# Attention beside linear attention: a tile transpose moved from TensorE and VectorE to the DMA engines, with another opening, another closing and one more block of exponentials on VectorE

## The chip, the cores and the metric

The kernel runs on one core of a Trainium2 chip. The metric is the device time of one execution in microseconds (us); the time before is the median of three runs. The profile is of one further execution, which has its own time.

## The reference

Two independent layers read a sequence of 2048 rows of width 640, with 32 heads of width 20, in bf16; their outputs are set side by side.

```python
# A: softmax attention, no mask
q, k, v = split(x @ wqkv)                       # 32 heads of 20
p = softmax(q @ k.T * 20 ** -0.5)               # per head 2048 x 2048
a = concat_heads(p @ v) @ wo
# B: linear attention, phi(t) = where(t > 0, t + 1, exp(t)) + 1e-6
kv, z = phi(k).T @ v, phi(k).sum(0)             # per head 20 x 20 and 20
o = (phi(q) @ kv) / (phi(q) @ z + 1e-6)
b = concat_heads(o) @ wo
out = concat([a, b], -1)                        # 2048 x 1280
```

## The kernel before

**A.** The scores are cut into blocks of 128 keys by 512 queries of one head, written key-major into a PSUM bank. Four heads form a head group (8 of them) and four stretches of 512 queries a sequence, so there are 32 chunks, numbered n; a chunk has 16 key tiles kt of four blocks each, and four blocks of one key tile are a quad. The exponential of a block is done in one of two ways. Most go to ScalarE (`emit_exp`, L1266), which takes three and then two blocks from PSUM in one instruction; each such set is a group, numbered j, and `SB` has the two sets of banks, 0 to 2 and 3 to 4, that it alternates between. The others go to VectorE (`d_score`): a scale per block (L1301), then three polynomial steps for each pair of blocks (L1312, L1316, L1320). The table `ND` says for each chunk how many of its 16 quads VectorE takes; it sums to 56 of 512. `LEAD` says how far ahead of its chunk, in chunk lengths, VectorE begins. The product with V adds up in bank `PVB` over the 16 key tiles of a chunk; `norm` then divides by the row sum and puts the result in `OTp`, from where DMAs on the queue of SyncE (SP) carry it to `OTd`, the operand of the output product.

**B** and all projections are background steps (`_Step`): some matmuls into bank 6 or 7 and an evacuation. In the last part of B each tile t of 128 rows goes through `ndstep` (numerator and denominator of both halves of the heads; VectorE divides, L1719 and L1722, and writes the normalised rows to `o`, a part of tile `f_pk`), `trstep` (five TensorE transposes of 128 x 128 into PSUM, L1734, and one VectorE copy to `oT`, another part of `f_pk`, L1744) and `ostep` (the product of `oT` with `woB`, a part of `f_wBkv`, and the store of the rows).

**Order.** The program is straight-line code. A planner (`_Clock`) runs while it is generated: each operation has a modelled cost, and it picks the order in which steps, scores and VectorE operations are emitted for each engine. On the chip each engine runs its list in that order and waits on semaphores; TensorE in particular takes nothing out of turn. Idle stretches of TensorE are padded with products of zeros (`f_g`, `f_z` in the views), and the start with products of a constant (`warm_up`).

**Opening.** `start_loads` brings the first 512 rows of x as they are (tile `f_st`, two DMAs of 256 rows), pieces of the weights `f_wA`, and the other 1536 rows by DMA transposes from DRAM (15 of 512 x 128). `consts` transposes the first 512 rows on TensorE (L1070), copied to `f_xT` by VectorE and ScalarE. Q and K of the first chunk follow, and then the first scores.

**Closing.** After the last V product, the last `norm` gives `OTp`, which meets the weights of the last head group, `wo7`. The last 512 rows are eight half tiles. For those not in `LATE` the product of the other heads was done before and lies in `part`, added by VectorE (L1550); for those in `LATE`, `part1` puts it in a free bank after the last V product, `part2` adds the last group's share, and ScalarE copies the sum (L1546). The stores go out at L1537.

Of the kernel before, what the change touches and what calls it, by code (L numbers as in the profile page):

```python
# [6 lines left out]
BF16 = mybir.dt.bfloat16  # L7
# [8 lines left out]
D_MODEL = 640  # L16
# [711 lines left out]
class _Clock:  # L728
# [5 lines left out]
    def __init__(self):  # L734
        self.t = {"act": 2.0, "dve": 0.0, "pool": 0.0, "sp": 1.0}
        self.issue = 0.0
        self.mode = None
        self.tile = {}
        self.hist = []
# [60 lines left out]
class _Fast:  # L800
# [11 lines left out]
    LEAD = 0.6  # L812
    LATE = ((3, 1), (3, 0), (2, 1))
    ND = (1, 2, 2, 1, 2, 2, 1, 2, 2, 2, 2, 2, 2, 2, 1, 2, 2, 2, 2, 2, 2, 2, 1, 1, 2, 2, 2, 2, 2, 1, 2, 1)
# [208 lines left out]
    def start_loads(self):  # L1023
# [5 lines left out]
        for k in range(2):  # L1029
            sch.dma("sp", lambda e, k=k: e.dma_start(  # L1030
                xn[:, 2 * k:2 * k + 2, :], x2[256 * k:256 * (k + 1), :].rearrange("(t p) d -> p t d", p=128)),
                writes=tuple(("xn", t) for t in (2 * k, 2 * k + 1)), cost=(0.1, 3.5))
# [3 lines left out]
        def load(q, part):  # L1036
            a, b, res = part
            sch.dma(q, lambda e: e.dma_start(self.wA[:, :, a:b], awq[:, :, a:b]), writes=(res,),
                    cost=(0.5, 5.0 if b - a < 200 else 8.0))
# [3 lines left out]
        load("act", parts[0])  # L1043
        load("act", parts[1])
        load("sp", parts[2])
        for tc in range(1, self.NQC):
            for c in range(N_DC):
                sch.dma("sp", lambda e, c=c, tc=tc: e.dma_start_transpose(
                    self.xT[:, c, 512 * tc:512 * (tc + 1)], x2[512 * tc:512 * (tc + 1), 128 * c:128 * (c + 1)]),
                    writes=(("xT", c, tc),), cost=(1.65, 2.0))  # L1050
# [8 lines left out]
    def consts(self):  # L1059
# [6 lines left out]
        for half in range(2):  # L1066
            for c in range(N_DC):
                pb = ps[:, c, :].bitcast(BF16)
                for t in (2 * half, 2 * half + 1):
                    sch.op("pe", lambda e, c=c, t=t, pb=pb: e.transpose(  # L1070
                        pb[:, 128 * t:128 * (t + 1)], self.stage[:, t, 128 * c:128 * (c + 1)], self.ident[:]),
                        reads=(("xn", t), "ident"), writes=(("ps", c),), inc=(t == 3), cost=("f", 0, 128))
            if half == 0:
                self.warm_up(2)
        self.warm_up(2)
# [53 lines left out]
    def step_qk(self, which, g, tc):  # L1129
# [20 lines left out]
        def post(b):  # L1150
# [5 lines left out]
            if g == 0 and tc == 0 and which == "Q":  # L1156
                return sch.op("act", lambda e: e.copy(dst, ps[:, b, :]), reads=(("ps", b),), writes=(res,),
                              cost=0.5).t
            if which == "K" and tc == 0:
                res = (res, ("K0", g % 2))  # L1160
                if g == 0:
                    self.dve(0.29, lambda e: e.tensor_copy(dst[:, 0:128], ps[:, b, 0:128]), reads=(("ps", b),),  # L1162
                             writes=(("K0", 0),))
                    return self.dve(0.56, lambda e: e.tensor_copy(dst[:, 128:512], ps[:, b, 128:512]),  # L1164
                                    reads=(("ps", b),), writes=(("K", 0, 0),)).t
            else:
                res = (res,)
# [68 lines left out]

    def force_qk(self, n, kt):
        g, qc = divmod(n, self.NQC)
        self.force(("Q", g, qc))
        self.force(("K", g, kt // 4))  # L1240
# [10 lines left out]
    def ahead(self, j):  # L1251
        for n, kt, i in self.groups[min(j + 4, len(self.groups) - 1)]:
            self.force_qk(n, kt)
# [251 lines left out]
    def finish_out(self):  # L1505
# [6 lines left out]
        banks = dict(zip(tiles, (6, 7, 3, 4, self.PVB, 0, 1, 2)))  # L1512

        def part1(x):
            for c in range(N_DC):
                self.out_round(banks[x], t0 + x[0], slice(320 * x[1], 320 * x[1] + 320), c, c == 0, False, True)
# [23 lines left out]
        for k in range(len(tiles) - len(late)):  # L1540
            for x in tiles[k:k + 1] + late[k:k + 1]:
# [43 lines left out]
    def b_steps(self):  # L1585
# [113 lines left out]
        def ndstep(t, h):  # L1699
# [15 lines left out]
            def post(b):  # L1715
# [8 lines left out]
                         writes=(("o", k, h),) + tuple(("pk", tl2, h2) for tl2 in range(4) for h2 in range(2)))  # L1724
            needs = tuple(("bq", tc, c) for c in cs) + (("bkv", NQC - 1, 3),)
            return _Step(mms, post, needs=needs, key=("nd", t, h), cols=2352)

        def trstep(t):
            k = t % 2

            def mms(b):
                pb = ps[:, b, :].bitcast(BF16)
                for c in range(N_DC):
                    sch.op("pe", lambda e, c=c: e.transpose(pb[:, 128 * c:128 * (c + 1)],  # L1734
                                                            self.o[:, k, 128 * c:128 * (c + 1)],
                                                            self.ident[:]),
                           reads=(("o", k, 0), ("o", k, 1), "ident"), writes=(("ps", b),), inc=(c == N_DC - 1),
                           cost=("f", 0, 128))
                    yield 128

            def post(b):
                pb = ps[:, b, :].bitcast(BF16)
                dst = self.oT[:, k].rearrange("p c m -> p (c m)")
# [316 lines left out]
```

## Time and profile before

| | |
|---|---|
| three runs | 870.16, 871.74, 871.98 us; median 871.74 |
| profiled execution | 870.36 us, of which the span is 868.5 |
| ScalarE busy | 850.1 us, 98% of the span |
| VectorE busy | 751.0 us, 86% |
| TensorE busy | 767.9 us, 88% (padding included) |
| first and last exponential on ScalarE | 10.57 to 858.12 us |

Times in the rows count from the start of the span. PE is TensorE's matmuls, PEld its weight loads, DVE VectorE, ACT ScalarE, SP SyncE; a name with q (SPq, ACTq) is the engine's sequencer, which issues DMAs. In a row of the timeline the first two numbers are start and length in us, and the bracket says how long the engine stood idle before it and for whom.

### The profile page before, as it was taken

What the parts mean: (1) busy time and instruction counts of PE and PEld (TensorE: products, weight loads), DVE (VectorE), ACT (ScalarE), POOL (GpSimd) and SP (SyncE); (2) the same over time, 40 slices, a digit from 0 to 9 for tenths busy, and PEclk for the clock granted to TensorE, in tenths of its full rate; (3) what the DMA queues carried; (4) which work ended last, traced back from release to release, by engine and by line L of the source; (5) the groups of instructions that cost most, each with busy time, mean ns of one, the idle gap of its engine ahead of it and who ended that gap; (6) DMA issues with size and microseconds to landing.
All of it is one profiled execution on the core that took longest, in us unless ns stands there. A gap on an engine that the chain in (4) does not pass through costs nothing.

```text
span 868.5 us, 25388 instructions
## 1 busy us (share of the span) xinstructions
PE 767.9 (88%) x11524; PEld 278.2 (32%) x11524; DVE 751.0 (86%) x1036; ACT 850.1 (98%) x790; POOL 50.9 (6%) x54
## 2 busy tenths in 40 slices
PE   8989888888888998888898999889988888899996
PEld 3333333322333333333332333223322332233342
DVE  6798899878989988998989999998779989898973
ACT  6999999999999999999999999999999999999995
POOL 4000000000000000000000000000000000000000
PEclk9999999999999999999999999999999999999999
DMA  6910001000020010000040000200010000001011
GB/s 130 248 44 5 5 6 32 5 6 6 18 59 3 5 36 6 6 3 3 6 73 6 5 13 19 43 5 14 28 32 5 5 22 21 3 4 44 21 45 65
DMA packets 45748, 24.01 MB, mean 28 GB/s; under 512 B 33985, under 2 KB 44993, under 8 KB 45633
## 3 DMA queue, kind: packets, MB, share of 16 engines
q1 hardware_dynamic: 44176, 21.92, 10.5%
q8 instruction: 92, 1.51, 0.8%
q10 hardware_dynamic: 1456, 0.40, 0.2%
q14 instruction: 24, 0.19, 0.1%
HBM read 7.31 MB, written 5.24 MB: 14 GB/s over the span
## 4 chain that ended last, share of the span: by engine, by line
ACT 95%; PE 4%; DVE 0%; issue 0%; ACTq 0%
ACT f_PT L1266 93%; PE ps L179 4%; ACT f_ex L1570 2%; ACT f_st L1546 0%; PE ps L1070 0%; DVE f_T L1414 0%; DVE f_OTp L1431 0%; DVE f_KT L1164 0%; DVE f_Tn L1427 0%; DVE f_OTp L1041 0%; ACTq L1537 0%; DVE f_KT L1162 0%; DVE f_R L1421 0%; DVE f_warm L1040 0%; ACTq L104 0%
## 5 line engine op out<-in xcount | busy, mean ns | idle before, releaser
L1266 ACT ACTIVATE f_PT<-ps 128x1536 bf16<-128x1536 f32 x730 | 841.4, 1423 | 3.6 <-PE ps L179 3.6
L179 PE MATMUL ps<-f_Qr,f_KT 20*128 20x512 bf16 x2048 | 302.6, 385 | 91.6 <-ACT f_PT L1266 82.3
L179 PE MATMUL ps<-f_g,f_z 32*128 32x512 bf16 (+3 forms) x1008 | 208.5, 378 | 0.0
L1301 DVE TENSOR_SCALAR f_W<-ps 128x512 f32<-128x512 f32 x224 | 154.0, 688 | 53.3 <-PE ps L179 50.5
L179 PEld LDWEIGHTS ps<-f_Qr,f_KT 20*128 20x128 bf16 x2048 | 75.0, 91 | 333.3 <-ACT f_PT L1266 315.4
L179 PE MATMUL ps<-f_PT,f_V 128*21 128x512 bf16 x1824 | 180.6, 387 | 0.8 <-ACT f_PT L1266 0.6
L1312 DVE SCALAR_TENSOR_TENSOR f_PL<-f_W 128x1024 f32<-128x1024 uint16 x112 | 136.2, 1216 | 1.1
L1316 DVE SCALAR_TENSOR_TENSOR f_PL<-f_W,f_PL 128x1024 f32<-128x1024 uint16 x112 | 136.0, 1214 | 1.1
L1320 DVE SCALAR_TENSOR_TENSOR f_PD<-f_PL,f_W 128x1024 uint16<-128x1024 f32 x112 | 135.6, 1211 | 0.6
L179 PE MATMUL ps<-f_xT,f_wA 128*32 128x512 bf16 x1280 | 88.9, 381 | 0.0
L1424 POOL TENSOR_TENSOR f_Tn<-f_T,f_R 128x320 bf16<-128x320 f32 x31 | 41.3, 1331 | 782.8 <-DVE f_R L1421 782.8
L179 PEld LDWEIGHTS ps<-f_PT,f_V 128*21 128x21 bf16 x1824 | 44.5, 89 | 101.0 <-issue 97.5
L179 PE MATMUL ps<-f_wBkv,f_xB 128*32 128x320 bf16 x1280 | 60.4, 303 | 0.0
L179 PEld LDWEIGHTS ps<-f_g,f_z 128*32 128x32 bf16 (+1 forms) x1008 | 51.4, 93 | 12.5 <-issue 8.8
L179 PEld LDWEIGHTS ps<-f_xT,f_wA 128*32 128x32 bf16 x1280 | 30.2, 95 | 30.8 <-issue 9.8
L1467 DVE CAST f_st<-ps 128x320 bf16<-128x320 f32 x56 | 27.2, 487 | 13.9 <-PE ps L179 12.7
L179 PEld LDWEIGHTS ps<-f_wBkv,f_xB 128*32 128x32 bf16 x1280 | 31.1, 97 | 18.6 <-issue 5.5
L1570 ACT ACTIVATE f_ex<-ps 128x320 f32<-128x320 f32 (+1 forms) x52 | 36.3, 698 | 0.0
L179 PE MATMUL ps<-f_wBkv,f_pk 128*32 128x320 bf16 x640 | 30.7, 300 | 0.0
L179 PE MATMUL ps<-f_wA,f_OTd 128*32 128x320 bf16 (+1 forms) x640 | 30.6, 301 | 0.1
L179 PE MATMUL ps<-f_wA,f_xT 128*32 128x160 bf16 (+1 forms) x640 | 29.6, 301 | 0.4
L179 PE MATMUL ps<-f_kvm,f_cs 128*32 128x336 bf16 x384 | 29.1, 306 | 0.0
(88 smaller groups left out, 508.6 us busy)
## 6 DMA issues: line engine op xcount, KB each, us to landing
out_dram<-f_st SPq DMA_DIRECT2D x31, 160.0 KB
f_OTd<-f_OTp SPq DMA_DIRECT2D x108, 20.0 KB
f_wBkv<-in_B_wqkv_dram SPq DMA_DIRECT2D x1, 1600.0 KB
f_wA<-in_A_wqkv_dram SPq DMA_DIRECT2D x2, 685.0 KB
f_wBq<-in_B_wqkv_dram SPq DMA_DIRECT2D x1, 800.0 KB
f_wA<-in_A_wo_dram SPq DMA_DIRECT2D x1, 800.0 KB
f_wBkv<-in_B_wo_dram SPq DMA_DIRECT2D x1, 800.0 KB
f_st<-in_A_x_dram SPq DMA_DIRECT2D x2, 320.0 KB
```

The costliest lines, as they stand in the source:

```text
L179: lambda e: e.matmul(out, lhsT, rhs, start=start, stop=stop, tile_position=tp, skip_group_check=sgc),
L1266: sch.op("act", lambda e: e.activation(self.PT[:, s0:s0 + n, :], ps[:, b0:b0 + n, :], AF.Exp, bias=(self.OCT + self.EXP_S) * LN2, scale=sc ...
L1301: self.dve(0.69, lambda e: e.tensor_scalar(dst, ps[:, b, :], cs, cb, op0=ALU.mult, op1=ALU.add), reads=(("ps", b),), writes=(("W", x, h),))
L1312: self.dve(1.24, lambda e: e.scalar_tensor_tensor(pl, lo, self.EXP_A, lo, op0=ALU.add, op1=ALU.mult), reads=rw, writes=(("PL", x),), fill= ...
L1316: self.dve(1.24, lambda e: e.scalar_tensor_tensor(pl, lo, self.EXP_B, pl, op0=ALU.add, op1=ALU.mult), reads=rw, writes=(("PL", x),), fill= ...
L1320: self.dve(1.24, lambda e: e.scalar_tensor_tensor(pd, pl, self.EXP_K, w, op0=ALU.mult, op1=ALU.add), reads=rw + (("PL", x),), writes=(("PD ...
L1424: sch.op("pool", lambda e: e.tensor_tensor(n3[:, :, 0:D_HEAD], t3[:, :, 0:D_HEAD], rb, op=ALU.mult), reads=("T1", ("R", n % 2)), writes=(" ...
L1467: self.dve(0.49, lambda e: e.tensor_copy(dst, src), reads=reads, writes=writes)
L1570: sch.op("act", lambda e: e.activation(ex, src, AF.Exp, bias=-1.0), reads=(("ps", b),), writes=(("ex", k),), cost=0.05 + 0.00084 * n)
```

## The change

Six edits:

1. `trstep` is gone. When VectorE has written the second half of `o` for a tile, five DMA transposes of 128 x 128 are issued on SP's queue, from `o` to `oT`, both in on-chip memory. `ostep` waits for each fifth by itself. The planner reckons 0.4 us of SP's queue for each and 2.5 us until it has landed.
2. `ND` sums to 57: one more quad goes to VectorE, 4 blocks fewer to ScalarE. Chunk 0 has none now, and chunk 4 has three. `LEAD` is 0.75.
3. The loads at the start are spread: the second half of the first x rows on ScalarE's queue, the piece of K's weights on SP's, the piece of V's weights behind two of the transposes.
4. The four `warm_up` products between and behind the first transposes are gone, and these run by column block.
5. A function `opening` writes the first projections out: all of Q, then the first 128 keys of K, part of the other keys, the scores of group 0, then the rest.
6. `LATE` has four half tiles. All four `part1` come ahead of the `part2`, and the last copies and stores alternate between VectorE and ScalarE.

```diff
-    LATE = ((3, 1), (3, 0), (2, 1))
-    ND = (1, 2, 2, 1, 2, 2, 1, 2, ...
+    LATE = ((3, 1), (3, 0), (2, 1), (2, 0))
+    ND = (0, 2, 2, 1, 3, 2, 0, 2, ...
...
-        for k in range(2):
-            sch.dma("sp", lambda e, k=k: e.dma_start(
+        for k, q in enumerate(("sp", "act")):
+            sch.dma(q, lambda e, k=k: e.dma_start(
...
-        load("act", parts[0])
-        load("act", parts[1])
-        load("sp", parts[2])
+        load("act", parts[0], 2.5)
+        load("sp", parts[1], 3.6)
...
+    def opening(self):
+        rounds("wq", "Q", 6, 0, 512, range(N_DC))
+        self.done[("Q", 0, 0)] = sch.op("act", lambda e: e.copy(self.Qr[:, 0, :], ps[:, 6, :]), ...
+        rounds("wk", "K", 7, 0, 128, range(N_DC))
+        kt = self.KT[:, 0, 0:512]
+        self.dve(0.29, lambda e: e.tensor_copy(kt[:, 0:128], ps[:, 7, 0:128]), ...
+        rounds("wk", "K", 5, 128, 512, range(2))
+        self.emit_scores(0)
+        rounds("wk", "K", 5, 128, 512, range(2, N_DC))
+        self.done[("K", 0, 0)] = self.dve(0.56, lambda e: e.tensor_copy(kt[:, 128:512], ps[:, 5, 128:512]), ...
...
-        for x in late[:2]:
-            part1(x)
-        for x in tiles[:len(tiles) - len(late)]:
-            part2(x)
-        for x in late[:2]:
-            part2(x)
-        for x in late[2:]:
-            part1(x)
-            part2(x)
+        for x in late:
+            for c in range(N_DC):
+                self.out_round(banks[x], t0 + x[0], ...
+        for x, y in zip(tiles, late):
+            part2(x)
+            part2(y)
...
-        def trstep(t):
...
+        def transpose(t):
             k = t % 2
+            for c in range(N_DC):
+                sch.dma("sp", lambda e, c=c: e.dma_start_transpose(
+                    self.oT[:, k, c, :], self.o[:, k, 128 * c:128 * (c + 1)]),
+                    reads=(("o", k, 0), ("o", k, 1)), writes=(("oT", k, c),), cost=(0.4, 2.5))
+            self.done[("tr", t)] = self.ck.t["sp"] + 2.5
...
-            order = [("n", 0), ("n", 1), ("t", 0), ("n", 2), ("o", 0), ("t", 1), ("n", 3), ("o", 1),
-                     ("t", 2), ("o", 2), ("t", 3), ("o", 3)]
+            order = [("n", 0), ("n", 1), ("o", 0), ("n", 2), ("o", 1), ("n", 3), ("o", 2), ("o", 3)]
```

Three places in the order of TensorE's instructions. In them `f_xT,f_wA` is a projection of Q or K, `f_Qr,f_KT` a score block, `f_PT,f_V` and `f_PD,f_V` the product with V of blocks from ScalarE and from VectorE. The first place is the start of the program, before:

```order
L179 MATMUL ps<-f_OTp 128x512 x8
L1070 MATMUL ps<-f_id,f_st 128x128 x10
L179 MATMUL ps<-f_OTp 128x512 x2
L1070 MATMUL ps<-f_id,f_st 128x128 x10
L179 MATMUL ps<-f_OTp 128x512 x2
L179 MATMUL ps<-f_xT,f_wA 32x512 x40
L179 MATMUL ps<-f_Qr,f_KT 128x512 x5
```

The same place with the change:

```order
L179 MATMUL ps<-f_OTp 128x512 x8
L1069 MATMUL ps<-f_id,f_st 128x128 x20
L179 MATMUL ps<-f_xT,f_wA 32x512 x20
L179 MATMUL ps<-f_xT,f_wA 32x128 x20
L179 MATMUL ps<-f_xT,f_wA 32x384 x8
L179 MATMUL ps<-f_Qr,f_KT 128x512 x3
L179 MATMUL ps<-f_xT,f_wA 32x384 x12
L179 MATMUL ps<-f_Qr,f_KT 128x512 x2
```

The scores of the first group (x3) now stand behind 20 + 20 + 8 projections, of which 28 are short, and no longer behind 40 long ones. The second place is in B's last part with the change, around the first matmul of `ostep` for tile t = 3 (`f_wBkv,f_pk` is the output product, its first x8 row that of tile 2, its x16 row that of tile 3):

```order
L179 MATMUL ps<-f_wBkv,f_pk 32x320 x20
L179 MATMUL ps<-f_Qr,f_KT 128x512
L179 MATMUL ps<-f_g,f_z 128x512
L179 MATMUL ps<-f_Qr,f_KT 128x512 x2
L179 MATMUL ps<-f_wBkv,f_pk 32x320 x8
L179 MATMUL ps<-f_Qr,f_KT 128x512
L179 MATMUL ps<-f_g,f_z 128x512
L179 MATMUL ps<-f_Qr,f_KT 128x512
L179 MATMUL ps<-f_PT,f_V 21x512 x4
L179 MATMUL ps<-f_wBkv,f_pk 32x320 x16
```

No transpose stands on TensorE any more; the x16 row waits for DMAs, and scores for ScalarE stand right behind it. Counted over the whole list, the score blocks between the last `ndstep` matmul of a tile and its first `ostep` matmul are, for t = 0 to 15: 19, 34, 50, 16, 22, 49, 33, 28, 19, 34, 46, 17, 28, 36, 102 and 113 (of 2048 in the program). The third place is the closing, before:

```order
L179 MATMUL ps<-f_PT,f_V 21x512 x8
L179 MATMUL ps<-f_wA,f_OTd 32x320 x40
L179 MATMUL ps<-f_wo,f_OTp 32x320 x28
L179 MATMUL ps<-f_wA,f_OTd 32x320 x20
L179 MATMUL ps<-f_wo,f_OTp 32x320 x4
```

The same place with the change:

```order
L179 MATMUL ps<-f_wA,f_OTd 32x320 x20
L179 MATMUL ps<-f_PT,f_V 21x512 x8
L179 MATMUL ps<-f_wA,f_OTd 32x320 x80
L179 MATMUL ps<-f_wo,f_OTp 32x320 x32
```

Between the last V product and the first use of `OTp` stand 80 matmuls now, not 40.

More of the change, by code (lines that the diff above doesn't have):

```diff
@@ L1511, in finish_out @@
         tiles = [x for x in tiles if x not in late] + late
[L1512 to L1516, printed above, removed]
+        last = (len(self.groups) - 1) % 2
+        lb = tuple(self.SB[1 - last]) + tuple(self.SB[last])
+        banks = dict(zip(tiles, (6, 7, self.PVB, lb[4]) + lb[:4]))
         def part2(x):
```

95 lines of the change are left out of this document (41 added, 54 removed).

## The prediction

> **What bounds the kernel now.** The page comes first: the busy times, the chain that ended last, and the costliest group.
>
> ```profile
> PE 767.9 (88%) x11524; PEld 278.2 (32%) x11524; DVE 751.0 (86%) x1036; ACT 850.1 (98%) x790; POOL 50.9 (6%) x54
> ACT 95%; PE 4%; DVE 0%; issue 0%; ACTq 0%
> L1266 ACT ACTIVATE f_PT<-ps 128x1536 bf16<-128x1536 f32 x730 | 841.4, 1423 | 3.6 <-PE ps L179 3.6
> ```
>
> ScalarE works for 98% of the span and is 95% of the chain, nearly all of it in the 730 exponentials. Before them it was idle for only 3.6 us. So three things can move the end: when the first exponential starts, how much ScalarE has to do until the last, and what follows the last. The chain in order of time gives the three stages and the price of a group (the mean of eight, alternating three and two blocks).
>
> ```profile
> 10.57 6.89 ACT f_PT L1266 x6
> 453.44 9.04 ACT f_PT L1266 x8
> 810.88 47.24 ACT f_PT L1266 x42
> 858.12 0.04 issue
> ```
>
> The opening takes 10.57 us, the stream of exponentials 847.5, the closing 868.5 - 858.1 = 10.4. A group costs 9.04 / 8 = 1.13 us for 2.5 blocks, so a block costs 0.452 us. A matmul or a VectorE operation that is removed is worth something only where ScalarE waits for it.
>
> **The opening.** The timeline of its first 11 us:
>
> ```profile
> 0.74 0.97 SPq L1030 DMA_DIRECT2D f_st<-in_A_x_dram  x2
> 1.49 3.40 PE L179 MATMUL ps<-f_OTp 128*128 128x512 bf16 x8 [1.49 <-DVE f_OTp L1041]
> 4.72 0.72 PE L1070 MATMUL ps<-f_id,f_st 128*128 128x128 bf16 x10
> 5.61 0.65 PEld L1070 LDWEIGHTS ps<-f_id,f_st 128*128 128x128 bf16 x10 [0.23 <-DMA f_st<-in_A_x_dram]
> 5.71 0.72 PE L1070 MATMUL ps<-f_id,f_st 128*128 128x128 bf16 x10
> 6.80 2.34 PE L179 MATMUL ps<-f_xT,f_wA 128*32 128x512 bf16 x40
> 8.11 0.59 ACT L1157 CAST f_Qr<-ps 128x512 bf16<-128x512 f32 x1 [0.90 <-PE ps L179]
> 9.52 0.56 DVE L1164 CAST f_KT<-ps 128x384 bf16<-128x384 f32 x1
> 10.13 0.60 PE L179 MATMUL ps<-f_Qr,f_KT 20*128 20x512 bf16 x5 [0.99 <-DVE f_KT L1164]
> 10.57 17.50 ACT L1266 ACTIVATE f_PT<-ps 128x1536 bf16<-128x1536 f32 x15 [1.87 <-PE ps L179]
> ```
>
> The second half of x landed at about 5.6. Its transposes, 40 projections (all of Q and K) and the copy of the remaining 384 keys then follow one another, and TensorE stands idle for 0.99 us until the copy ends at 10.08. With the change the first group needs only the first 128 keys, since chunk 0 gives no block to VectorE. Group 0 so waits for Q's copy and a copy of 128 columns.
>
> When do the x rows land? The stretches by microsecond, whose last number is GB/s:
>
> ```profile
> 2.00:3.00 1.00, 1.00 (x4) 0.33 (x3) 1.00 (x1) 0.23 (x2) 1.00 (x2) 1.00 0.75 186
> 3.00:4.00 1.00, 1.00 (x3) 0.29 (x2) 0.88 (x1) 0.00 (x0) 1.00 (x4) 1.00 1.18 323
> 4.00:5.00 1.00, 1.00 (x8) 0.57 (x7) 0.00 (x0) 0.00 (x0) 1.00 (x6) 1.00 1.09 312
> ```
>
> Both halves are 655 KB. At 186 + 323 KB by 4.0 and 312 KB per us after that they need until about 4.5 us if nothing is ahead of them, which two queues with x first in each come near to (estimate). Where the weights still share the engines it stays at 5.6. From 4.72 on, 20 transposes take (0.72 - 0.22) / 9 = 0.056 us each (0.22 is the pipeline's own length) and end at 6.0; copies overlap them but for the last, so Q starts at 6.2. Half of 2.34 us later, at 7.45, ScalarE copies Q (0.59, to 8.15 with the wake-up). The 128-key projections and their copy end about then too. As before, 0.44 us lie between the score matmuls and the exponential (10.13 to 10.57): 8.2 + 0.44 = 8.6. With x at 5.6 it is 9.6. I take 8.8, nearer to the early end because x is first in both queues: **-1.8 us** (bounds -2.0 and -1.0). Against that, group 1 needs the remaining keys. Their last 12 matmuls run behind the first scores (8.8 + 0.5), then comes the 0.56 us copy and the scores again, some 10.45, while exponential 0 ends at 8.8 + 1.34: **+0.3 us**. The DMA transposes of the other rows come out no later than before, since only short issues are ahead of them.
>
> **The stream.** `ND` 57 for 56 takes four blocks from ScalarE, 4 x 0.452 = **-1.8 us**. What VectorE takes on and gives up:
>
> ```profile
> L1301 DVE TENSOR_SCALAR f_W<-ps 128x512 f32<-128x512 f32 x224 | 154.0, 688 | 53.3 <-PE ps L179 50.5
> L1312 DVE SCALAR_TENSOR_TENSOR f_PL<-f_W 128x1024 f32<-128x1024 uint16 x112 | 136.2, 1216 | 1.1
> L1722 DVE TENSOR_TENSOR f_pk<-ps,f_rd 128x320 bf16<-128x320 f32 x32 | 15.7, 492 | 1.1
> L1719 DVE RECIPROCAL f_rd<-ps 128x16 f32<-128x16 f32 x32 | 8.0, 250 | 2.0 <-PE ps L179 1.7
> L1744 DVE COPY f_pk<-ps 128x640 bf16<-128x640 bf16 x16 | 7.7, 484 | 1.7 <-PE ps L1734 1.7
> L1734 PE MATMUL ps<-f_id,f_pk 128*128 128x128 bf16 x80 | 8.3, 222 | 0.0
> ```
>
> A quad is 4 x 0.688 and three steps for two pairs, 6 x 1.216: 10.0 us. The 16 copies give back 7.7. VectorE gains 2.3 us on 868.5 - 751 = 117 us of idle time, which covers it: 0 in the sum. TensorE loses 80 transposes of its own padded time: 0 as well.
>
> The new wait is that of `ostep` on its DMAs, and TensorE takes nothing out of turn: behind its first matmul stand the scores of the next groups, and ScalarE has one group (1.13 us) at most before it waits too. No row shows a 128 x 128 transpose within the chip. The nearest are the transposes of B's rows from DRAM, the transposes of the opening, and the small on-chip copies of `OTp` (issue times least/median/most, ns; then one burst of five and the stretches in which its transfers end):
>
> ```profile
> L1558 SPq DMA_TRANSPOSE f_xB<-in_B_x_dram x40: 1132/1261/2198, 28.3 to 633.5; - x40
> L1443 SPq DMA_DIRECT2D f_OTd<-f_OTp x140: 554/707/1088, 42.9 to 839.3; - x140
> 2.26 21.19 SPq L1048 DMA_TRANSPOSE f_xT<-in_A_x_dram  x15
> 128.88 6.37 SPq L1558 DMA_TRANSPOSE f_xB<-in_B_x_dram  x5
> 136.00:136.50 0.50, 0.50 (x20) 0.20 (x12) 0.00 (x0) 0.50 (x2) 0.00 (x0) 1.00 0.35 71
> 136.50:137.00 0.50, 0.50 (x13) 0.15 (x12) 0.09 (x1) 0.50 (x2) 0.00 (x0) 1.00 0.00 0
> ```
>
> The burst was issued by 135.25 and moved its last bytes before 136.5, so a transpose lands 1.25 us after its issue. An issue of ours costs between 0.32 (a quarter of 1.26, being a quarter of the rows) and 1.41 (21.19 / 15). I take 0.8, near the on-chip copies, the only rows with that source. All five so land 5 x 0.8 + 1.25 = 5.25 us after `o` is ready, with 2.9 and 8.3 as ends.
>
> How long may they take? A score block stands for 847.5 / 2048 = 0.414 us of the stream. The tightest tile (t = 3) has 16 of them, 6.6 us, of which VectorE needs about 2.1 (one 1.2 us operation ahead, 0.25 + 0.49 for the division, the wake-ups); the fifth chunk of `oT` is read 0.6 later (a product of five chunks takes 0.9, see the closing). That leaves 5.1 us; the others among the five tightest (17, 19, 19, 22 blocks) have 5.5, 6.4, 6.4 and 7.6. At 5.25 the delay of 0.15 lies inside ScalarE's one group; I put **+0.3 us** for all tiles (bounds 0 and the slow rival's price below).
>
> For a 128 x 128 transpose the Trainium skill, "VectorE: DVE Perf Modes", section "The three transpose paths", gives 390 ns on TensorE and 1309 ns on the DMA path, and its rules advise TensorE where the destination may be PSUM. It speaks against this edit. By its price five in a row take 6.5 + 1.25 = 7.8 us, and the edit would cost about 4 us and not 0.3 (estimate from that page). No row of before decides it; the 1.26 us of a transpose four times as long makes me doubt it.
>
> **The closing.** Its rows:
>
> ```profile
> 858.16 0.59 PEld L179 LDWEIGHTS ps<-f_wA,f_OTd 128*32 128x32 bf16 x16
> 859.02 0.64 PEld L179 LDWEIGHTS ps<-f_wA,f_OTd 48*32 48x32 bf16 x20 [0.26 <-issue]
> 860.92 1.13 PE L179 MATMUL ps<-f_wo,f_OTp 128*32 128x320 bf16 x28 [0.68 <-DVE f_OTp L1431]
> 861.36 2.08 DVE L1550 TENSOR_TENSOR f_st<-ps,f_kvx 128x320 bf16<-128x320 f32 x5 [0.50 <-PE ps L179]
> 862.03 0.75 ACT L1546 CAST f_st<-ps 128x320 bf16<-128x320 f32 x2 [3.92 <-PE ps L179]
> 863.28 0.43 ACT L1546 CAST f_st<-ps 128x320 bf16<-128x320 f32 x1 [0.50 <-PE ps L179]
> L1537 SPq DMA_DIRECT2D out_dram<-f_st x3: 332/332/1757, 862.3 to 863.8; - x3
> ```
>
> TensorE waited 0.68 us for `OTp` before. A half tile of `part1` takes 0.9 us (859.02 - 858.16 and alike), so four end at 858.16 + 3.6 = 861.8 and the first `part2` starts 0.9 late: the cover is gone. VectorE then has four adds at 0.4 and ScalarE four copies at 0.38 with a store's issue between them, so the last copy ends at 864.4 and not 863.7. But the last store of before was held 1.76 us in its issue, from 863.8; others took 0.33. If the new last store, on ScalarE's queue, isn't held, the end comes 0.7 earlier, and if it is, 0.7 later. I can't tell which: **0**, bounds -0.7 and +0.7.
>
> **The sum** is -1.8 + 0.3 - 1.8 + 0.3 + 0 = -3.0 us. From the profiled execution's 870.36 us (its span and 1.86 around it) that gives 867.4. Its own runs' median is 1.4 higher, from which it would be 868.7; I predict 868.0, between the two. With the early bounds the sum is -2.0 + 0.3 - 1.8 + 0 - 0.7 = -4.2, so 866.2 from the profile.
>
> **Rivals.**
>
> *Late transposes (slower).* If an issue costs 1.41 us as in the opening, five land after 8.3 us. Over the room of the five tightest tiles, and less 0.9 us of ScalarE's cover, ScalarE loses 2.3 + 1.9 + 1.0 + 1.0 = 6.2 us: 868.0 - 0.3 + 6.2 = 873.9. From about 8.2 us for five on, the change is slower. For it: each tile's wait is on the one engine that feeds ScalarE. Against it: only these tiles are tight. Chance 0.14.
>
> *VectorE becomes the bound.* Chunk 4 has three quads, 30 us, in 1.75 chunk lengths (41 us) from its lead to its end; the rest of VectorE's work is (751 - 560) / 868.5 = 0.22 of the time, 9 us. That fits by 2 us only. If it fails, the V products of chunk 4 wait for VectorE and then ScalarE does, by 2 to 4 us: 870 to 872. The idle times above speak against it on average, not at this place. Chance 0.10.
>
> *A slow TensorE at the start.* The first eight products took 0.43 us each, half the speed of the later ones. Four products that kept it busy are gone; if Q, K and the scores run at that speed, they take 1.6 us more and most of the opening's gain is lost: 869.6. Against it: before, 0.99 us of idling at 9.1 was followed by full speed. Chance 0.06. The Trainium skill, "TensorE: Matmul & The Clock Gate", Part 1, says that full clock comes after about 3.4 us of sustained work, in a window whose phase differs from run to run; by that rule this rival could come in some runs and not in others, and one trace can't show it.
>
> **Chances.** The forecast has 0.66 and spans 866.2 to 870. Left over are 0.04 for a cost I don't see. About 0.2% (1.74 us) is what a measurement of this kernel can tell from no change, so faster means under 870.0 and slower over 873.5. Faster: 0.64 of the forecast, 0.04 of the slow start, 0.02 of VectorE: 0.70. Within: 0.02, 0.02, 0.07, and 0.05 of the late transposes: 0.16. Slower: the remaining 0.14. The range is 866.0 to 873.0: it takes in the early bounds, VectorE's rival and the milder half of late transposes.
>
> **What would show it.** In the profile after: the first exponential at 8.6 to 9.6; 728 exponentials; idle time of ScalarE before them, apart from the opening, of under 3 us; issues of the new transposes near 0.8 us; no wait of TensorE on `f_pk` before an output product of B; the first product with `wo7` 3.6 us after the last V product. The forecast is wrong if ScalarE's idle time in the last 380 us grows by several us, with TensorE at those places waiting for `f_pk`, or if the exponentials of the fifth chunk wait for `f_PD`.

## The result, and the profile with the change

| | before | with the change |
|---|---|---|
| median of eleven runs | 871.48 us | 873.78 us |
| lowest and highest | 870.16, 874.12 | 872.45, 881.41 |
| profiled execution, span | 870.36, 868.5 | 875.93, 874.1 |

The ratio of all runs is 1.0037, with an interval of 1.0020 to 1.0054: slower by 2.3 us by the medians and 3.2 by the ratio, where 3 to 4 us faster were forecast. The executions of one kernel spread over several us here, and the longest have the lowest mean TensorE clock (with the change 872.45 us at 0.994 of full speed, 881.41 at 0.981). The profiled one had 0.987, so its 875.93 us shows more of the loss than the median does.

The page, in the lines that answer to those of before (busy times, chain, costliest group), and the group of B's output products:

```profile
PE 768.8 (88%) x11429; PEld 275.3 (31%) x11429; DVE 751.9 (86%) x1028; ACT 849.4 (97%) x789; POOL 50.1 (6%) x54
ACT 87%; PE 7%; DMA 2%; SPq 2%; DVE 1%; issue 0%; ACTq 0%; DVEq 0%
L1275 ACT ACTIVATE f_PT<-ps 128x1536 bf16<-128x1536 f32 x728 | 839.4, 1416 | 10.5 <-PE ps L179 10.3
L179 PE MATMUL ps<-f_wBkv,f_pk 128*32 128x320 bf16 x640 | 31.9, 307 | 4.0 <-DMA f_pk<-f_pk 3.9
```

ScalarE has two exponentials fewer and 2.0 us less of them (839.4 for 841.4), as was meant. But it stood idle before them for 10.5 us and not 3.6, and the chain now runs through DMAs and SP's queue. The output products waited 3.9 us for transposes. The exponentials with their gaps, from ScalarE's timeline (the first two are the opening; the rows left out begin after gaps of 0.7 us or less):

```profile
9.02 1.45 ACT L1275 ACTIVATE f_PT<-ps 128x1536 bf16<-128x1536 f32 x1 [0.58 <-PE ps L179]
10.67 38.85 ACT L1275 ACTIVATE f_PT<-ps 128x1024 bf16<-128x1024 f32 x34 [0.20 <-PE ps L179]
73.16 1.45 ACT L1275 ACTIVATE f_PT<-ps 128x1536 bf16<-128x1536 f32 x1 [1.06 <-PE ps L179]
...
80.20 3.71 ACT L1275 ACTIVATE f_PT<-ps 128x1536 bf16<-128x1536 f32 x3 [1.39 <-PE ps L179]
...
525.24 2.37 ACT L1275 ACTIVATE f_PT<-ps 128x1536 bf16<-128x1536 f32 x2 [2.42 <-PE ps L179]
528.57 2.37 ACT L1275 ACTIVATE f_PT<-ps 128x1536 bf16<-128x1536 f32 x2 [0.97 <-PE ps L179]
531.68 2.36 ACT L1275 ACTIVATE f_PT<-ps 128x1536 bf16<-128x1536 f32 x2 [0.74 <-PE ps L179]
...
849.97 13.66 ACT L1275 ACTIVATE f_PT<-ps 128x1536 bf16<-128x1536 f32 x12 [0.25 <-PE ps L179]
```

The stream starts at 9.02 and ends at 863.63: 854.6 us, where 847.5 - 1.8 were forecast. Its largest hole is at 522 to 532 us, 2.42 + 0.97 + 0.74 = 4.1 us of ScalarE. It is tile t = 3 of B, the tightest one. What happened there (issue of the transposes, then TensorE's products; the x12 are three chunks of the output product, the first x4 the fourth chunk, the second the fifth):

```profile
516.52 6.92 SPq L1737 DMA_TRANSPOSE f_pk<-f_pk  x5
521.24 0.58 PE L179 MATMUL ps<-f_wBkv,f_pk 128*32 128x320 bf16 x12
524.18 0.46 PE L179 MATMUL ps<-f_wBkv,f_pk 128*32 128x320 bf16 x4 [2.36 <-DMA f_pk<-f_pk]
525.51 0.48 PE L179 MATMUL ps<-f_wBkv,f_pk 128*32 128x320 bf16 x4
```

VectorE had written `o` by 516.5, and TensorE had the first three chunks done by 521.8. The fourth could be read only at 524.1, 7.6 us after `o`, and in the 2.36 us from 521.8 on no score was made. The issues over the whole program (least, median, most, ns), and TensorE's clock around the place (the last three numbers are the granted clock, the DMA share and GB/s):

```profile
L1737 SPq DMA_TRANSPOSE f_pk<-f_pk x80: 1094/1232/2542, 482.1 to 798.2; - x80
```

```profile
520.00:522.00 2.00, 1.81 (x31) 0.72 (x27) 2.00 (x6) 2.00 (x3) 0.34 (x1) 1.00 0.15 33
522.00:524.00 2.00, 0.00 (x0) 0.00 (x0) 0.66 (x1) 0.81 (x1) 1.24 (x1) 0.94 0.12 25
524.00:526.00 2.00, 1.82 (x19) 0.43 (x19) 0.00 (x0) 0.77 (x1) 0.00 (x0) 0.50 0.23 82
526.00:528.00 2.00, 2.00 (x26) 0.72 (x26) 1.11 (x2) 1.60 (x2) 0.00 (x0) 0.50 0.02 4
528.00:530.00 2.00, 2.00 (x19) 0.42 (x23) 1.94 (x3) 1.43 (x2) 0.00 (x0) 0.50 0.08 21
```

An issue took 1.23 us at the median, not 0.8, and one of them 2.5. By the semaphores in the trace, 67 of the 80 transposes landed 1.09 to 1.20 us after the end of their issue and 13 only 1.85 to 2.84 us after it. During each of these 13, and during each of the 14 issues of over 1.5 us, a 16 KB packet of another kind was moving, which the DMA view calls `instruction`. The fourth transpose of tile 3 is one of the 13: 15 of its 16 parts had landed by 522.56, the last at 524.14. The DMA view of 521.5 to 524.2 us has one such packet (packets, MB, share of the DMA engines' time); it moved from 522.12 to 523.05:

```profile
q8 instruction: 1, 0.02, 2.1%
```

So about 0.7 of the 2.36 us are the price of the issues, and 1.6 are this delay. That the packet caused it is inferred from the times; no run takes the packet away.

Towards the end of the wait, at 523.77, TensorE's clock fell to half for 6.8 us, and ScalarE, supplied by it, had the second and the third gap there.

### The profile page after: what moved, and what is told of

The parts are those of the page before. It is cut to its first block, busy times and chain, and to the rows that moved or that the text cites. A ratio compares the mean times of both kernels' runs of the same rounds, so it can differ in the third digit from the quotient of the medians.

```text
span 874.1 us, 25300 instructions
## 1 busy us (share of the span) xinstructions
PE 768.8 (88%) x11429; PEld 275.3 (31%) x11429; DVE 751.9 (86%) x1028; ACT 849.4 (97%) x789; POOL 50.1 (6%) x54
## 4 chain that ended last, share of the span: by engine, by line
ACT 87%; PE 7%; DMA 2%; SPq 2%; DVE 1%; issue 0%; ACTq 0%; DVEq 0%
ACT f_PT L1275 84%; PE ps L179 7%; ACT f_ex L1574 2%; SPq L1737 1%; DMA f_pk<-f_pk 1%; DMA f_wA<-in_A_wqkv_dram 1%; SPq L1452 0%; DMA f_OTd<-f_OTp 0%; DVE f_W L1310 0%; DVE f_PL L1325 0%; ACT f_st L1550 0%; DVE f_pk L1726 0%; DVE f_OTp L1440 0%; DVE f_PD L1329 0%; DVE f_PL L1321 0%
## 5 line engine op out<-in xcount | busy, mean ns | idle before, releaser
L1275 ACT ACTIVATE f_PT<-ps 128x1536 bf16<-128x1536 f32 x728 | 839.4, 1416 | 10.5 <-PE ps L179 10.3
L179 PE MATMUL ps<-f_Qr,f_KT 20*128 20x512 bf16 x2048 | 306.8, 388 | 91.2 <-ACT f_PT L1275 82.4
L1310 DVE TENSOR_SCALAR f_W<-ps 128x512 f32<-128x512 f32 x228 | 156.5, 687 | 50.5 <-PE ps L179 48.2
L1321 DVE SCALAR_TENSOR_TENSOR f_PL<-f_W 128x1024 f32<-128x1024 uint16 x114 | 138.3, 1215 | 0.7
L1329 DVE SCALAR_TENSOR_TENSOR f_PD<-f_PL,f_W 128x1024 uint16<-128x1024 f32 x114 | 138.4, 1214 | 0.4
L1325 DVE SCALAR_TENSOR_TENSOR f_PL<-f_W,f_PL 128x1024 f32<-128x1024 uint16 x114 | 138.1, 1213 | 0.7
L179 PE MATMUL ps<-f_xT,f_wA 128*32 128x512 bf16 (+2 forms) x1300 | 90.7, 377 | 0.3 <-DMA f_wA<-in_A_wqkv_dram 0.3
L179 PE MATMUL ps<-f_kvm,f_wBkv 128*32 128x336 bf16 x384 | 29.0, 307 | 0.0
```

Of the source, the lines that this page charges most:

```text
L179: lambda e: e.matmul(out, lhsT, rhs, start=start, stop=stop, tile_position=tp, skip_group_check=sgc),
L1275: sch.op("act", lambda e: e.activation(self.PT[:, s0:s0 + n, :], ps[:, b0:b0 + n, :], AF.Exp, bias=(self.OCT + self.EXP_S) * LN2, scale=sc ...
L1310: self.dve(0.69, lambda e: e.tensor_scalar(dst, ps[:, b, :], cs, cb, op0=ALU.mult, op1=ALU.add), reads=(("ps", b),), writes=(("W", x, h),))
L1321: self.dve(1.24, lambda e: e.scalar_tensor_tensor(pl, lo, self.EXP_A, lo, op0=ALU.add, op1=ALU.mult), reads=rw, writes=(("PL", x),), fill= ...
L1325: self.dve(1.24, lambda e: e.scalar_tensor_tensor(pl, lo, self.EXP_B, pl, op0=ALU.add, op1=ALU.mult), reads=rw, writes=(("PL", x),), fill= ...
L1329: self.dve(1.24, lambda e: e.scalar_tensor_tensor(pd, pl, self.EXP_K, w, op0=ALU.mult, op1=ALU.add), reads=rw + (("PL", x),), writes=(("PD ...
```

## The experiments

The theory after this: the loss is the wait for transposes that issue at 1.23 us, made larger by the half clock behind it. The rivals: a gain that was never there (opening, closing, 57th quad), or VectorE as the new bound. In all experiments the time of the kernel before, on the same chip, was 871.6 to 872.1 us.

### The same order without the waits

The cleanest one. Every engine keeps its list, and all DMAs are issued; only the output product of B reads a constant (`ident`) in place of `oT`, so B's half of the output isn't computed.

```diff
-                    self.cmm(ps[:, b, 0:320], self.oT[:, k, c, :], self.woB[...
+                    self.cmm(ps[:, b, 0:320], self.ident, self.woB[...
```

> The changed kernel in the same order of every engine, its DMA transposes issued as before, but the output product of B reads a constant tile and not their result (the B half of the output is not computed). This takes the wait away and leaves the transposes. My theory: the stretch from 510 to 535 us loses its 4 us of ScalarE idling and its half clock, 869 to 870.5, and the early stretch (70 to 80 us) stays as it is. Rival (traffic and queue, not the wait): 873 to 874.

869.65 us, ratio 0.9969 [0.9952, 0.9985]. Tile 3 in its timeline, and the clock in the two stretches behind the place:

```profile
514.51 6.21 SPq L1737 DMA_TRANSPOSE f_pk<-f_pk  x5
519.23 0.72 PE L179 MATMUL ps<-f_wBkv,f_id 128*32 128x320 bf16 x16
520.48 0.31 PE L179 MATMUL ps<-f_wBkv,f_id 128*32 128x320 bf16 x4
```

```profile
522.00:524.00 2.00, 1.64 (x27) 0.63 (x27) 2.00 (x4) 2.00 (x3) 0.00 (x0) 1.00 0.30 91
524.00:526.00 2.00, 2.00 (x35) 0.54 (x27) 0.50 (x1) 2.00 (x3) 0.00 (x0) 1.00 0.09 22
```

TensorE has the five chunks of the first half done 6.3 us after the first issue, at full clock, and ScalarE is busy without a gap. By the medians the waits cost 873.78 - 869.65 = 4.1 us; by the two ratios, 1.0037 and 0.9969, 5.9. The transposes are still issued here, and the fourth of tile 3 lands late here too (3.0 us after its issue), but nothing waits for them.

### The planner told the measured price

```diff
-                    reads=(("o", k, 0), ("o", k, 1)), writes=(("oT", k, c),), cost=(0.4, 2.5))
+                    reads=(("o", k, 0), ("o", k, 1)), writes=(("oT", k, c),), cost=(1.25, 2.5))
```

> The changed kernel, with the planner told that a tile transpose holds SP's queue for 1.25 us and not 0.4 (the profile after shows 1.23); the planner then puts the output product later (24 score blocks at the tightest tile and not 16). My theory: the waits of TensorE on the transposes vanish (9.7 us of PE and PEld waits on f_pk fall under 1) and with them some 4 us: about 870. Rival, the transposes disturb in another way (the queue, other DMAs): no gain, 873 to 874.

870.09 us, ratio 0.9993 [0.9975, 1.0012]. No instruction waits for `f_pk<-f_pk` any more; the planner puts more scores between a tile and its output product. The loss is gone, but no gain over before can be told from it. Its profile has the first exponential at 10.96 us, of which more below.

### Edits undone or alone

Edit 1 undone (transposes on TensorE again, 57 quads, new opening and closing), and edit 1 alone on the kernel before:

```diff
-                if h == 1:
-                    transpose(t)
+            order = [("n", 0), ("n", 1), ("t", 0), ("n", 2), ("o", 0), ("t", 1), ...
```

> The changed kernel with edit 1 undone: tile transposes on TensorE and VectorE again, all other edits kept. My theory: the changed kernel loses (a) about 4 us of ScalarE's time behind one late group of DMA transposes, tile 3, at 516 to 532 us, where TensorE waits 2.4 us and then runs at half clock, and (b) about 4 us to slow stretches of TensorE in the re-planned order (70 to 80 us at clock 0.50, 94 to 101 us), which no DMA transpose touches. Then this one is about 870 us, 4 below the changed kernel, and its early stretch (60 to 105 us) still shows ScalarE idle for 2 to 4 us if that part is from the ND table. Rival: the transposes are innocent and the new ND table costs it all; then it stays at 872 to 874.

885.35 us, ratio 1.0177 [1.0154, 1.0200]: missed by 15 us.

> The kernel before with edit 1 alone. My theory: it loses what the late transposes cost, by the room of its tiles (20 score blocks at the tightest two) 2 to 5 us: 873 to 876. If the transposes are innocent: 871 to 872.

889.01 us, ratio 1.0219 [1.0195, 1.0244]: missed by 13 us. Of the first, TensorE's waits; of the second, SP's queue and what it held (the row of `f_wA,f_OTd` is an output product of A, which needs the copies issued at 848.64):

```profile
PEld ps L179 <- DVE f_PD L1329: 10.2, 9, 2.8
PE ps L179 <- DVE f_PD L1329: 7.6, 6, 2.5
```

```profile
841.51 7.08 SPq L1733 DMA_TRANSPOSE f_pk<-f_pk  x5
848.64 3.00 SPq L1443 DMA_DIRECT2D f_OTd<-f_OTp  x4
852.98 0.72 PE L179 MATMUL ps<-f_wA,f_OTd 128*32 128x320 bf16 x8 [5.68 <-DMA f_OTd<-f_OTp]
854.30 2.48 ACT L1266 ACTIVATE f_PT<-ps 128x1536 bf16<-128x1536 f32 x2 [6.06 <-PE ps L179]
```

In the second kernel `OTp` was ready at 843.8, but five transposes stood on the queue ahead of its four copies; TensorE stood 5.7 us for these and ScalarE 6.1 us for TensorE. To see how much of this is the wrong price, edit 1 alone once more, with 1.25 for 0.4 as above:

> The kernel before with edit 1 alone (transposes by DMA), the planner told 1.25 us of queue time for each. At 0.4 us it took 889 us. Theory (the loss comes from the wrong price, by which products and copies were placed behind transposes that had not landed): no waits on f_pk and none of more than 1 us on f_OTd, and 871.5 us, the time of before. Rival (the DMA queue itself can't carry 80 transposes beside its other work): over 880 us with waits on f_OTd or f_pk again.

875.02 us, ratio 1.0038 [1.0020, 1.0056]. The right price is worth 14 us, and waits on DMAs for `f_pk` and `f_OTd` are gone. But 3 us remain, where the theory had none: its waits are on `f_PD` (at most 1.9 us), two of ScalarE's larger gaps lie in a stretch at half clock, 467 to 473 us, and its first exponential came at 11.56, 1.0 us later than before, in an opening that this edit leaves alone.

The two kernels with TensorE transposes and 56 quads: first the new opening and closing on the kernel before (edits 3 to 6), then edit 1 undone with chunk 4 at two quads.

> The kernel before with the new opening and the new closing alone: 56 quads on VectorE, the transposes on TensorE. The run with edit 1 undone took 885 us, with TensorE waiting 18 us for VectorE's exponentials and B unfinished when the exponentials ended. My theory: that was the 57th quad without the 7.7 us that the DMA transposes give back to VectorE. With 56 quads these waits go and this is 870 to 872. Rival, any change of the start re-plans the whole program, and the tables fit only the plan that they were made for: 875 to 890 again.

873.02 us, ratio 1.0019 [1.0004, 1.0035]. The opening's gain is there and is given back at once:

```profile
9.12 1.45 ACT L1275 ACTIVATE f_PT<-ps 128x1536 bf16<-128x1536 f32 x1 [0.58 <-PE ps L179]
...
15.28 5.97 ACT L1275 ACTIVATE f_PT<-ps 128x1536 bf16<-128x1536 f32 x5 [1.23 <-PE ps L179]
22.03 25.88 ACT L1275 ACTIVATE f_PT<-ps 128x1024 bf16<-128x1024 f32 x23 [0.78 <-PE ps L179]
```

With the old table VectorE has blocks of chunk 0 among its first copies, and at 14.9 TensorE waits for its copy of K's next 512 keys. With the new table, which gives chunk 0 none, the next gap after 10.67 is at 73 us (above). So the opening seems to need edit 2's table; the table alone was not tried.

```diff
-    ND = (0, 2, 2, 1, 3, 2, 0, 2, ...
+    ND = (0, 2, 2, 1, 2, 2, 0, 2, ...
```

> The changed kernel with the transposes back on TensorE and VectorE's copy, and with 56 quads (chunk 4 has two instead of three): the new opening, the new closing and the new start of the table alone. Theory (with the copies back VectorE has no room for the 57th quad, which made the kernel with 57 and TensorE transposes 885 us): no waits on f_PD of more than 1 us, work of B ends before the closing, and 870 us (871.6 less the opening's 1.6). Rival (the 885 us came from the new table's order of chunks or from LEAD, not from VectorE's sum of work): it stays above 878 us.

878.23 us, ratio 1.0076 [1.0055, 1.0097]. And the same table on the kernel with the measured price, that is, one quad fewer on VectorE and nothing else:

> The changed kernel with the planner told 1.25 us for each transpose, and chunk 4 with two quads on VectorE instead of three (56 in all, 732 exponential instructions or nearly). Theory (ScalarE is the bound in the stream and VectorE has room once the 16 copies are gone): a quad more on ScalarE costs 1.8 us, 871.9 us against 870.1. Rival (VectorE is the bound around chunk 4): the same 870 us or less.

879.02 us, ratio 1.0111 [1.0078, 1.0145], where 871.9 was expected. Both theories of these two runs fell: taking work from VectorE made the kernel slower by 9 us, so neither ScalarE's 0.452 us per block nor VectorE's sum of work explains it. In its profile TensorE waits 3.4 us for `f_PD` at 784 us, and runs at half clock behind that and again through the closing:

```profile
PEld ps L179 <- DVE f_PD L1329: 4.4, 5, 3.4
```

```profile
786.00:788.00 2.00, 2.00 (x27) 0.72 (x19) 1.69 (x4) 1.67 (x2) 0.00 (x0) 0.50 0.00 0
...
864.00:866.00 2.00, 2.00 (x32) 0.79 (x29) 0.76 (x2) 0.00 (x0) 0.00 (x0) 0.50 0.00 0
```

```profile
785.30 2.37 ACT L1275 ACTIVATE f_PT<-ps 128x1024 bf16<-128x1024 f32 x2 [2.53 <-PE ps L179]
...
869.42 0.90 ACT L1550 CAST f_st<-ps 128x320 bf16<-128x320 f32 x2 [7.59 <-PE ps L179]
```

What these kernels have in common is that each edit makes the planner write another order over hundreds of us, and single places of it are then 2 to 6 us short. That this order makes the loss is argued, not tested. So these times say little on the edit that was undone. Only the run without the waits holds the order still, and I rest the split of the loss on it.

### Is the half clock the doing of the wait?

Products of zeros into the wait itself, 40 of them, first ahead of the fifth chunk of tile 3:

```diff
+                    if t == 3 and h == 0 and c == N_DC - 1:
+                        (40 products of f_g by f_z, added to the same bank)
```

> The changed kernel with 40 products of zeros (10 rounds of four, about 2.2 us) put on TensorE right ahead of the fifth chunk of tile 3's output product, where it otherwise stands idle for 2.4 us; every other instruction keeps its place. My theory: of the 4.8 us that ScalarE loses there, about 2.4 are the wait itself and 2.4 the half clock of TensorE that follows the idle stretch. With TensorE kept busy through the wait the clock stays at 1.00 from 522 to 532 us and ScalarE loses about 2.5 us and not 4.8: some 2 us below the changed kernel, 871.5 to 872. Rival, the clock has nothing to do with the idling: loss unchanged, 873.8, or more by the added products.

877.61 us, ratio 1.0063 [1.0040, 1.0086]. The wait was at the fourth chunk, ahead of the padding, which then ran at half clock itself (4.48 us for 40): the design failed. Put ahead of the fourth chunk (`c == 3`):

> The changed kernel, with 40 products of zeros put into TensorE's list ahead of tile 3's fourth chunk of the output product (first half), the point where TensorE stood idle for 2.4 us in the changed kernel. At full clock the 40 take 2.2 us, which is about the wait. If the drop of TensorE's clock to 0.50 after that wait comes from the idling, the clock between 524 and 532 us stays above 0.9, ScalarE's three gaps there (2.42 + 0.97 + 0.74 us) shrink to the first one alone, and the time is 872 us. If the drop has another cause, half clock and gaps stay, and the time is 873.8 us or a little more.

```profile
518.65 2.33 PE L179 MATMUL ps<-f_g,f_z 128*32 128x512 bf16 x40
520.81 0.31 PE L179 MATMUL ps<-f_wBkv,f_pk 128*32 128x320 bf16 x4
521.50 7.22 ACT L1275 ACTIVATE f_PT<-ps 128x1536 bf16<-128x1536 f32 x6 [1.68 <-PE ps L179]
```

```profile
520.00:522.00 2.00, 1.77 (x32) 0.57 (x24) 0.00 (x0) 0.50 (x1) 0.24 (x1) 1.00 0.28 91
522.00:524.00 2.00, 1.72 (x34) 0.77 (x34) 1.28 (x3) 1.97 (x2) 0.00 (x0) 1.00 0.00 0
524.00:526.00 2.00, 2.00 (x35) 0.71 (x32) 2.00 (x3) 1.91 (x2) 0.00 (x0) 1.00 0.05 14
```

At this place it came as expected: the products take 2.33 us where the wait took 2.36, so the scores behind them are held up as long, but the clock stays at 1.00, and one gap of 1.68 us is left of three with 4.1. (The fourth transpose had no late part in this execution; the fifth had, and TensorE waited 0.51 us for it.) So some 2.4 us of the hole were the half clock. Two other kernels idled at tile 3 without products there, the one with the padding at the fifth chunk and the one with the held memset alone (below), and half clock followed for 6.8 us in both. But the median is 875.13, ratio 1.0036 [1.0021, 1.0051], as with the change alone: in its profile the hole opened at another tile, at 704 to 713 us, with half clock, a wait of 1.35 us for `f_pk`, and gaps of 1.22, 0.43 and 1.32 us. Where the clock gives way differs from run to run, which the three gaps of the change at 73 to 80 us (1.06, 0.59 and 1.39 us) show too:

```profile
68.00:70.00 2.00, 1.04 (x15) 0.22 (x13) 2.00 (x4) 2.00 (x3) 0.90 (x1) 0.95 0.00 0
70.00:72.00 2.00, 2.00 (x26) 0.87 (x26) 1.41 (x3) 2.00 (x2) 0.68 (x1) 0.50 0.03 8
...
78.00:80.00 2.00, 2.00 (x30) 0.76 (x22) 0.85 (x2) 0.81 (x1) 0.00 (x0) 0.50 0.00 0
```

In the kernel with the measured price and a held memset (below), whose TensorE list is the same up to there, TensorE was as idle in these 2 us and kept its clock:

```profile
68.00:70.00 2.00, 0.98 (x18) 0.23 (x11) 2.00 (x6) 2.00 (x3) 0.10 (x1) 1.00 0.00 0
70.00:72.00 2.00, 2.00 (x39) 0.75 (x34) 1.98 (x3) 2.00 (x3) 1.48 (x1) 1.00 0.04 8
```

It lost it for 3 us at 95 us instead. There, behind a wait of 1.09 us for `f_PD`, I put 16 products, in the kernel with the measured price:

```diff
+        if j == 72:
+            self.pad(j)      # 16 products of f_g by f_z into bank PVB
```

> The changed kernel with the planner told 1.25 us, and 16 products of zeros (0.9 us at full clock) ahead of a V product of VectorE's blocks at about 95 us, where TensorE stood idle for 1.09 us and then ran at half clock for 3 us in the kernel without them. If idling of this size lets the clock drop, it stays above 0.95 between 90 and 100 us, ScalarE's gap of 0.98 us at 99 us goes, and the time is 0.5 to 1 us below 870.1. If not, the gap stays and the time is 870.1 us.

The clock stayed at 1.00 from 90 to 102 us, the gaps at 97 to 100 us went, and the profiled execution, at 867.39 us, is the fastest of this study. The median, 871.68, ratio 0.9994 [0.9979, 1.0009], did not move: the place was mended, the time was not.

### The opening and an earlier transpose

In the kernels without waits and with the measured price, the copy of the first 128 keys of K took 1.6 to 1.7 us and not 0.29, and ended with a memset on GpSimd:

```profile
4.87 2.34 PE L1069 MATMUL ps<-f_id,f_st 128*128 128x128 bf16 x20
7.46 2.90 POOL L1109 MEMSET f_kvm<- 128x3360 bf16 x1
8.73 1.71 DVE L1236 CAST f_KT<-ps 128x128 bf16<-128x128 f32 x1
10.96 1.45 ACT L1275 ACTIVATE f_PT<-ps 128x1536 bf16<-128x1536 f32 x1 [1.92 <-PE ps L179]
```

In them the 20 first transposes took 2.34 us, and 1.35 in the profile with the change, where the copy began at 8.14. The memset held back until that copy, with the change, and with the measured price as well:

```diff
+        sch.barrier(("pool",), (("K0", 0),))
         sch.op("pool", lambda e: e.memset(self.kvm[:], 0.0), ...
```

> The changed kernel, with GpSimd's long memset (f_kvm, 2.9 us from 7.5 on) held back until the copy of the first 128 keys is done. In two of four profiles with the new opening that copy took 1.6 us and not 0.29, ending just when the memset ended, and the first exponential came at 10.96 and not at 9.0 to 9.4. My theory: it never does with the memset held back: first exponential at or under 9.6 and the copy at 0.29, worth 0 to 1.6 us by run, 0.8 in the median: 873. Rival, another cause (TensorE's clock, weights landing late): the copy takes 1.6 us again or the first exponential is late without it.

> The changed kernel with the planner told 1.25 us of queue time for each transpose instead of 0.4, and with GpSimd's memset held back until the first 128 keys of K are copied. Theory (waits on the transposes cost 4 us, the disturbed copy at the start up to 1.5 us): no wait on f_pk, first exponential at 9.1 to 9.7, and 868.5 us. Rival (the opening's gain is always given back a little later, since K's other tiles and TensorE's clock set the pace up to 100 us): 870 us, as without the held memset.

874.26 us (ratio 1.0030 [1.0016, 1.0044]) and 870.98 us (0.9993 [0.9975, 1.0011]). The copy takes 0.29 us in both and the first exponential comes at 9.67 and 9.63, but the medians are those without the edit. Last, the memset held, two of the five transposes issued after the first half of `o`, and the planner told 1.25 us of queue and 1.2 us until the landing:

```diff
-                if h == 1:
-                    transpose(t)
+                transpose(t, h)      # chunks 0, 1 after half 0; 2, 3, 4 after half 1
```

> The changed kernel with the memset held back, with the first two of a tile's five transposes issued after the first half of the rows is written (so that three and not five stand between the whole tile and its last chunk), and the planner told 1.25 us of queue for each. My theory: three land 3 x 1.23 + 0.74 = 4.4 us after the tile is ready, no wait on them is left, and with the opening steady this is 868 to 869.5, about 2 to 3 under the kernel before. Rival: the queue of SP, which the transposes hold for 98 us in all, delays the copies to OTd instead, and TensorE waits there: 871 to 874.

872.53 us, ratio 1.0010 [0.9991, 1.0029]; its runs go from 868.77 (clock 0.996) to 875.69 (0.985). No wait on `f_pk`, and no gain over the plain right price.

## Why the prediction was wrong

**The step that failed** is the term of the new wait, "I take 0.8, near the on-chip copies, the only rows with that source", put at +0.3 us. The source did not set the price, the kind did: 1.232 us at the median, beside the 1.261 of the transposes four times as long. The quarter that I allowed for a quarter of the rows was not there at all. By the prediction's own formula, five so land 5 x 1.23 + 1.25 = 7.4 us after `o` and four 6.2, where 5.25 was reckoned for all five. At tile 3 the last landed after 8.0 us, and the fourth after 7.6, though 15 of its 16 parts were there after 6.0, as the formula has it. So the price alone accounts for about 0.7 us of the wait, which lies within the 0.9 us of ScalarE's cover; the other 1.6 us are the part that landed late beside an `instruction` packet, and the formula's 1.25 us for the landing had no room for it. The kernel with the change and the held memset shows the same two sizes: its fourth chunk of tile 3 waited 0.78 us without such a packet, its fifth 1.67 us with one. No run has the price without the packets, so how much each of them cost the median is open. The Trainium skill, "VectorE: DVE Perf Modes", section "The three transpose paths", gives 1309 ns for this transpose on the DMA path, from which the prediction worked out about 4 us. The issues agree with that figure (1.23 us). The loss to the waits, 4.1 us, is near that estimate and not near the 0.3, but partly by luck, since the estimate held neither the late part nor the clock.

**What no term held** is the clock. Less the 0.9 us of cover, 2.36 us of wait would cost ScalarE 1.5; it cost 4.1 in that profile, and 1.68 where TensorE was kept busy. The Trainium skill, "TensorE: Matmul & The Clock Gate", Part 1, has the clock judged in a free-running window of about 3.4 us. The traces agree. With the change half clock was granted from 69.80 to 80.04, 97.11 to 100.52 and 523.77 to 530.60 us: three, one and two times 3.41 us. In the traces of all sixteen kernels every change of the clock lies a whole number of 3.413 us from the first one, which comes at 4.57 us in one execution and at 7.35 in another. The stretch before 523.77 holds 1.95 us of idling, so a wait shorter than the window was enough; and the idling at 69 us, much the same with the change, with the right price and the held memset, and with the 16 products, falls differently into these stretches and led to half clock in the first alone. The prediction used this rule for the start alone.

**The rival of late transposes** gave 873.9 us, and 873.78 was measured. It had the right engine and sign. It priced four tiles at 6.2 us without the clock, and the trace has one large hole, with the clock and a late part, so the match is partly luck; its turning point, "about 8.2 us for five", took four tight tiles together, and in the profile one of them at 8.0 made 4.1 us of the loss.

**Point by point, the rest.** First exponential: 8.6 to 9.6 forecast, 9.02 in the profile with the change; but 10.96 in four others, so -1.6 us with a loss of up to 1.9 in some executions. The rival of a slow TensorE at the start came in part: the clock rose to full at 4.95 us in that profile, but at 6.91 to 7.35 us in seven others, and three of these, with the memset held, had the first exponential at 9.63 to 9.67, 0.6 us later and not 1.6. Group 1: +0.3 forecast, a gap of 0.20. Exponentials: 728, 2.0 us less of them. Closing: first product with `wo7` at 867.50, 3.8 after the last V product's start at 863.69; 10.5 us in all for 10.4, so the 0 was right. VectorE as the bound: no wait for `f_PD` over 1.4 us with the change, so not at chunk 4. Without the transposes' term the forecast was -3.3 us. The kernel without their waits stands at 0.9969 of before, -2.7 us, with -4.2 and -1.3 as ends (-2.0 by the medians): these terms, taken together, held. One by one the medians don't separate them.

**What stays open.** Why the kernels without any wait on transposes, but in another order, keep, by the ratios, 2 to 4 us less of this gain than the one in the same order; which share the clock's run-to-run places have in that; and whether the held copy at the start is rare in the timed runs or hidden later. No complete kernel was found that is faster than the one before by more than the measurement tells; the waits are avoided by the right price, at the same time as before.

## What to carry to other kernels

A DMA transpose is priced by the issue, not by its bytes: look for the nearest row of the same kind before one of the same source, and count its hold on the queue for everything behind it there. Leave room for a late landing too: here one in six came 0.7 to 1.7 us late. Where an engine feeds the bottleneck in strict order, a wait of 2 us can cost nearly twice that, because the clock drops behind it; see the granted clock after each wait, not its length alone. And where a planner writes the order, undoing one edit changes everything after it: an experiment that keeps every engine's list and changes one operand tells more than any that asks the planner again.

## What the runs showed of the hardware

- A 128 x 128 bf16 transpose within the chip holds SP's queue for 1.23 us (1.09 to 2.54), one of 512 x 128 from DRAM for 1.26: hardly a difference for four times the data.
- With the change, 67 of the 80 transposes landed 1.09 to 1.20 us after the end of their issue, 13 after 1.85 to 2.84 us. During each of the 13, and each of the 14 issues of over 1.5 us, a 16 KB `instruction` packet was moving.
- TensorE at half clock (0.50) for 6.8 us after an idle 2.36 us at 522 us, and for 10.2 us after about 1 us idle in 2 us at 69 us; in other executions the same idling at 69 us led to no drop. The clock changed only at steps of 3.413 us from its first change, in all sixteen traces.
- A VectorE copy of 128 x 128 took 0.29 us beside a GpSimd memset when it began at 8.14 to 8.51, or in the old opening at 9.19 and 9.47, and 1.6 to 1.7 us, to the memset's end, when it began at 8.70 to 8.82. Why those were held is not known.
